# Output blocks of a fused attention and MoE kernel, copied out of PSUM by halves

## The chip, the cores and the metric

The kernel runs on one core of one Trainium2 chip. The metric is the device time of one execution in microseconds (us). The engines are PE (matmul), DVE (vector), ACT (scalar), POOL and SP; SP and ACT can issue DMAs, and PSUM is the memory that PE accumulates in and that ACT and DVE read.

## The reference

Sparse attention feeds two feed-forward layers. The part that matters here is the last one, on 1536 tokens, with `w_in` 512 x 2048 and `w_out` 2048 x 512:

```python
def _moe2_ref(x, w_in, w_out):
    h = x @ w_in
    g = h * (1.0 / (1.0 + np.exp(-h)))
    return (g @ w_out).astype(np.float32)
```

## The kernel before

An order written out by hand (`ORDER`) runs the attention and the first layer. The second layer then runs in two groups of 768 tokens, `g` = 0 and 1. For each of 16 slices `m` of 128 hidden features `up(g, m)` makes the activated slice: `up_mm` (L560) runs 24 matmuls into one PSUM tile, ACT takes the tanh (L569), DVE multiplies (L575), and a pair of ACT (L110) and DVE (L111) copies splits the result into a high part `gh` and a low part `gl`. `down(g, m)` (L611) multiplies that slice by its rows of `w_out`. It runs 18 matmuls: three token blocks `t3`, two halves `s` of the group, and three products each. PE works one step ahead: `up(g, m)` stands ahead of `down(g, m-1)`.

The sums over all 16 slices stay in three PSUM tiles, `acc[g][t3]`, each of 128 partitions x 2 x 512 f32. Half `s` of block `t3` is `acc[g][t3][:, s]`, and it holds 128 rows of the output. In the last slice the order is t3 outside, s inside, so that one tile after the other is finished. When both halves of a tile are done, ACT copies half 0 (L620) and DVE half 1 (L618) into `x2T`, an SBUF tile that is free by then, both times 0.5, and SP issues one DMA of 256 KB for each (L621). That is three tiles, six copies and six DMAs in each group.

In group 0 this stands behind `x2split(1)`, which makes the input of group 1: four ACT copies (`x2_hi`, L540) and four DVE subtractions (`x2_lo`, L543). Behind group 0 stands `up(1, 0)`. Behind group 1 stands the end of the program: each engine takes a branch (L714) around a fallback that isn't run here, and then waits for the others.

The program is built by a framework that inserts the semaphore waits itself: a write to a tile waits for the earlier readers of that tile. The engines run their instructions in the order in which they were written.

Of the kernel before, what the change touches and what calls it, by code (L numbers as in the profile page):

```python
# [13 lines left out]
ACTF = mybir.ActivationFunctionType  # L14
ALU = mybir.AluOpType
# [41 lines left out]
def kernel(ctx, tc, q, k, v, n_global, n_local, w_in, w_out, g_ln, w2_in, w2_out, out):  # L57
    nc = tc.nc
    B, H, S, D = 2, 8, 768, 64
    NT, DM = out.shape  # L60
# [16 lines left out]
    x2T = per.tile([128, KD, NT], F32, name="x2T")  # L77
# [28 lines left out]
    def psum():  # L106
        return ps.tile([128, 2, 512], F32, tag="p", name="p")
# [409 lines left out]
    G = 768  # L517
    HG = 384
    NG = NT // G
# [10 lines left out]
    for i in range(NP):  # L530
# [4 lines left out]
        for j in range(2):  # L535
            r = (2 * i + j) * 128
# [61 lines left out]
    acc = {}  # L598

    def down(g, m):  # L600
        if m == 0:
            acc[g] = [psum() for _ in range(G // 256)]
        last = m == KF2 - 1
        gx = [gs.pop((g, m, s)) for s in range(2)]
        ST = [(s, t3) for t3 in range(3) for s in range(2)] if last else [(s, t3) for s in range(2) for t3 in range(3)]
        for s, t3 in ST:
            hi, lo = gx[s]
            o = acc[g][t3][:, s]
            c = slice(t3 * 128, (t3 + 1) * 128)
            for i, (x, w) in enumerate(((hi, w3h), (hi, w3l), (lo, w3h))):  # L610
                nc.tensor.matmul(o, lhsT=x[:, c], rhs=w[m // 2][:, m % 2, :], start=(m == 0 and i == 0), stop=(last and i == 2))  # L611
            if last and s:
                for h in range(2):
                    r = g * G + (3 * h + t3) * 128
                    o = acc[g][t3][:, h]
                    y = x2T[:, r // 384, r // 128 % 3 * DM:(r // 128 % 3 + 1) * DM]
                    if h:
                        nc.vector.tensor_scalar(out=y, in0=o, scalar1=0.5, scalar2=None, op0=ALU.mult)  # L618
                    else:
                        nc.scalar.activation(out=y, in_=o, func=ACTF.Copy, scale=0.5)  # L620
                    nc.sync.dma_start(out=out[r:r + 128, :], in_=y)  # L621

    def guard():
        V = nc.vector
# [53 lines left out]
    with tc.manual_schedule():  # L678
# [18 lines left out]
        for i in range(2, NP):  # L697
            w2alloc(w2b, i)
        bg(2)
        down(0, 0)  # L700
        for m in range(2, KF2):
            up(0, m, 2)
            down(0, m - 1)
        x2split(1)
        down(0, KF2 - 1)
        for m in range(KF2):
            up(1, m)
# [6 lines left out]
    with tc.If(fast == 0):  # L714
# [12 lines left out]
        with tc.tile_pool(name="ga", bufs=1, side="left") as ga:  # L727
# [17 lines left out]
            with tc.For_i(0, B, 1) as bi, tc.For_i(0, H, 1) as hi:  # L745
                t3 = ga.tile([128, TB, D], F32, name="gv")
# [9 lines left out]
                for qb in range(TB):  # L756
# [31 lines left out]
                    o = psum()[:, 0, 0:D]  # L788
# [115 lines left out]
```

## Time and profile before

| | us |
|---|---|
| median of 3 runs | 517.35 (517.03 to 517.89) |
| the profiled execution | 515.7 |
| its span, from the first to the last instruction | 513.9 |
| PE busy in it | 485.1 (94%) |
| DVE, ACT, POOL busy in it | 312.6, 254.3, 111.9 |

The span is 1.8 us shorter than the time of the same execution, and that execution was 1.65 us faster than the median. A row of the timeline gives the start, the duration, the engine, the line, the operation and the tiles; what stands in brackets is the idle time ahead of it and what ended that. Ends of matmuls are modelled.

### The profile page before, as it was taken

What the parts mean: (1) busy time and instruction counts of PE and PEld (TensorE: products, weight loads), DVE (VectorE), ACT (ScalarE), POOL (GpSimd) and SP (SyncE); (2) the same over time, 40 slices, a digit from 0 to 9 for tenths busy, and PEclk for the clock granted to TensorE, in tenths of its full rate; (3) what the DMA queues carried; (4) which work ended last, traced back from release to release, by engine and by line L of the source; (5) the groups of instructions that cost most, each with busy time, mean ns of one, the idle gap of its engine ahead of it and who ended that gap; (6) DMA issues with size and microseconds to landing.
All of it is one profiled execution on the core that took longest, in us unless ns stands there. A gap on an engine that the chain in (4) does not pass through costs nothing.

```text
span 513.9 us, 8122 instructions
## 1 busy us (share of the span) xinstructions
PE 485.1 (94%) x3028; PEld 432.4 (84%) x3028; DVE 312.6 (61%) x735; ACT 254.3 (49%) x580; POOL 111.9 (22%) x150
## 2 busy tenths in 40 slices
PE   2598999999999999999999999999999999999993
PEld 1376779889888998799989899998899899999982
DVE  5799999956585686862688989893541313222231
ACT  3798997765666575442254545443431222222121
POOL 3675333311012133320223333332000000000000
PEclk9989999999999999999999999999999999999997
DMA  8757251612111210200333333300020000000003
GB/s 263 243 153 218 86 165 42 226 43 82 29 36 43 102 42 12 73 14 30 94 113 122 124 128 119 122 2 0 21 103 1 0 1 0 1 1 1 0 1 129
DMA packets 26179, 38.36 MB, mean 75 GB/s; under 512 B 1548, under 2 KB 13844, under 8 KB 26132
## 3 DMA queue, kind: packets, MB, share of 16 engines
q1 hardware_dynamic: 24932, 36.71, 22.0%
q10 hardware_dynamic: 1200, 1.05, 0.7%
q8 instruction: 26, 0.43, 0.3%
q14 instruction: 21, 0.17, 0.1%
HBM read 34.61 MB, written 3.15 MB: 73 GB/s over the span
## 4 chain that ended last, share of the span: by engine, by line
PE 85%; DVE 8%; DMA 2%; ACT 1%; issue 1%; POOL 0%; SPq 0%; DVEq 0%
PE p L560 26%; PE p L611 26%; PE p L497 12%; PE p L413 9%; PE p L308 4%; PE p L355 3%; PE p L374 3%; PE p L477 2%; DVE A L327 2%; DMA rq<-in_q_dram 1%; DMA rk<-in_k_dram 1%; DVE cc L147 1%; DVE cc L145 1%; DVE cc L143 1%; ACT A L333 1%
## 5 line engine op out<-in xcount | busy, mean ns | idle before, releaser
L575 DVE SCALAR_TENSOR_TENSOR e<-e,p 128x384 f32<-128x384 f32 x64 | 32.6, 551 | 127.5 <-ACT e L569 127.5
L569 ACT ACTIVATE e<-p 128x384 f32<-128x384 f32 x64 | 28.0, 490 | 129.5 <-PE p L560 129.5
L611 PE MATMUL p<-w3h,gl 128*128 128x512 f32 x192 | 75.3, 392 | 0.0
L611 PE MATMUL p<-w3l,gh 128*128 128x512 f32 x192 | 75.2, 392 | 0.0
L611 PE MATMUL p<-w3h,gh 128*128 128x512 f32 x192 | 74.7, 389 | 0.0
L147 DVE SCALAR_TENSOR_TENSOR cc<-cx,cc 128x512 uint32<-128x512 uint32 x48 | 60.9, 1270 | 0.3
L560 PE MATMUL p<-x2h,w2h 128*128 128x384 f32 x256 | 55.2, 337 | 0.0
L560 PE MATMUL p<-x2l,w2h 128*128 128x384 f32 x256 | 55.0, 335 | 0.0
L560 PE MATMUL p<-x2h,w2l 128*128 128x384 f32 x256 | 54.7, 334 | 0.0
L333 ACT ACTIVATE A<-A,negmax 128x256 f32<-128x256 f32 (+1 forms) x96 | 46.0, 481 | 13.3 <-DVE negmax L327 11.7
L413 PE MATMUL p<-wih,xT 128*128 128x512 f32 x192 | 50.6, 405 | 0.5 <-DVE negmax L327 0.5
L327 DVE CUSTOM_DVE_ANT_0 A<-p,bias 128x256 f32<-128x256 f32 (+1 forms) x96 | 34.3, 395 | 23.1 <-PE p L355 14.6
L560 PEld LDWEIGHTS p<-x2h,w2h 128*128 128x128 f32 x256 | 45.6, 188 | 2.3
L560 PEld LDWEIGHTS p<-x2l,w2h 128*128 128x128 f32 x256 | 45.9, 188 | 0.0
L560 PEld LDWEIGHTS p<-x2h,w2l 128*128 128x128 f32 x256 | 45.3, 188 | 0.0
L611 PEld LDWEIGHTS p<-w3h,gl 128*128 128x128 f32 x192 | 36.0, 188 | 7.6
L611 PEld LDWEIGHTS p<-w3l,gh 128*128 128x128 f32 x192 | 36.0, 188 | 6.9
L611 PEld LDWEIGHTS p<-w3h,gh 128*128 128x128 f32 x192 | 36.1, 188 | 6.8
L413 PEld LDWEIGHTS p<-wih,xT 128*128 128x128 f32 x192 | 34.3, 189 | 8.5 <-DVE negmax L327 0.9
L110 ACT ACTIVATE gh<-e 128x384 fp32r<-128x384 f32 x60 | 29.7, 526 | 18.6 <-DVE e L575 18.6
L145 DVE SCALAR_TENSOR_TENSOR cc<-cx,cc 128x512 uint32<-128x512 uint32 x48 | 34.1, 716 | 0.0
L111 DVE TENSOR_TENSOR gl<-e,gh 128x384 fp32r<-128x384 f32 x60 | 30.8, 555 | 3.8
(117 smaller groups left out, 804.9 us busy)
## 6 DMA issues: line engine op xcount, KB each, us to landing
cx<-in_moe_w_out_dram SPq DMA_DIRECT2D x24, 512.0 KB, 3.4
cx<-in_moe_w_in_dram SPq DMA_DIRECT2D x23, 512.0 KB, 3.7
rq<-in_q_dram SPq DMA_DIRECT2D x12, 256.0 KB, 6.1
vf<-in_v_dram SPq DMA_DIRECT2D x12, 256.0 KB, 4.5
out_dram<-x2T SPq DMA_DIRECT2D x12, 256.0 KB, 2.7
rk<-in_k_dram SPq DMA_DIRECT2D x10, 256.0 KB, 5.6
rk<-in_k_dram ACTq DMA_DIRECT2D x2, 256.0 KB, 4.8
cx<-in_moe_w_in_dram ACTq DMA_DIRECT2D x1, 512.0 KB, 6.2
```

The source lines that it names most:

```text
L110: nc.scalar.activation(out=hi, in_=src, func=ACTF.Copy)
L111: nc.vector.tensor_tensor(out=lo, in0=src, in1=f(hi), op=ALU.subtract)
L145: V.scalar_tensor_tensor(out=y, in0=x[:, :, 0].bitcast(U32), scalar=29, in1=y, op0=ALU.logical_shift_right, op1=ALU.bitwise_or)
L147: V.scalar_tensor_tensor(out=y, in0=x[:, :, 1].bitcast(U32), scalar=0x80000000, in1=y, op0=ALU.bitwise_and, op1=ALU.bitwise_or)
L327: nc.vector.tensor_tensor_reduce(out=x[:, c, 0:n], in0=p[:, a, j, 0:n], in1=bb, scale=-0.125, scalar=1e30, op0=ALU.add, op1=ALU.min, accum ...
L333: nc.scalar.activation(out=x[:, c, 0:n], in_=x[:, c, 0:n], func=ACTF.Exp, bias=negmax[:, t * H + h:t * H + h + 1], scale=-1.0, accum_out=s ...
L413: nc.tensor.matmul(p[:, half, :], lhsT=x[:, a, kk, :], rhs=w[:, kk, n], start=(i == 0), stop=(i == 11))
L497: nc.tensor.matmul(p[:, d], lhsT=x[:, kk, c], rhs=y[:, kk, sl], start=(i == 0), stop=(i == 3 * KF - 1))
L560: nc.tensor.matmul(p, lhsT=w[m // 2][:, kk, c], rhs=x[:, kk, s * HG:(s + 1) * HG], start=(i == 0), stop=(i == 11))
L569: nc.scalar.activation(out=e, in_=p2[:, s, 0:HG], func=ACTF.Tanh, scale=0.5)
L575: nc.vector.scalar_tensor_tensor(out=e, in0=e, scalar=1.0, in1=p2[:, s, 0:HG], op0=ALU.add, op1=ALU.mult)
L611: nc.tensor.matmul(o, lhsT=x[:, c], rhs=w[m // 2][:, m % 2, :], start=(m == 0 and i == 0), stop=(last and i == 2))
```

## The change

In the last slice each half is copied right after its own three matmuls. Half 0 goes to ACT and half 1 to DVE, as before. The very last half of the program (group 1, t3 = 2, s = 1) is cut by columns: ACT copies the first 256, DVE the other 256. A DMA is issued by ACT where ACT copied and by SP where DVE copied. The number of DMAs goes from 12 to 13.

```diff
-            if last and s:
-                for h in range(2):
-                    r = g * G + (3 * h + t3) * 128
-                    o = acc[g][t3][:, h]
-                    y = x2T[:, r // 384, r // 128 % 3 * DM:(r // 128 % 3 + 1) * DM]
-                    if h:
-                        nc.vector.tensor_scalar(out=y, in0=o, scalar1=0.5, scalar2=None, op0=ALU.mult)
+            if last:
+                end = g == NG - 1 and t3 == 2 and s == 1
+                r = g * G + (3 * s + t3) * 128
+                y = x2T[:, r // 384, r // 128 % 3 * DM:(r // 128 % 3 + 1) * DM]
+                for n, act in ((slice(0, 256), True), (slice(256, DM), False)) if end else ((slice(0, DM), s == 0),):
+                    if act:
+                        nc.scalar.activation(out=y[:, n], in_=o[:, n], func=ACTF.Copy, scale=0.5)
                     else:
-                        nc.scalar.activation(out=y, in_=o, func=ACTF.Copy, scale=0.5)
-                    nc.sync.dma_start(out=out[r:r + 128, :], in_=y)
+                        nc.vector.tensor_scalar(out=y[:, n], in0=o[:, n], scalar1=0.5, scalar2=None, op0=ALU.mult)
+                    (nc.scalar if act else nc.sync).dma_start(out=out[r:r + 128, n], in_=y[:, n])
```

On PE, in the last slice of group 1, tile t3 = 1 (`p_3966`; `gh_4753` and `gl_4754` belong to half 0, `gh_4757` and `gl_4758` to half 1):

```order
 L611 MATMUL p_3966<-w3l7_2820,gh_4753 128x512
 L611 MATMUL p_3966<-w3h7_2819,gl_4754 128x512
-L611 MATMUL p_3966<-w3h7_2819,gh_4757 128x512
+L611 MATMUL p_3966<-w3h7_2819,gh_4757 128x512 [waits Activation_49]
 L611 MATMUL p_3966<-w3l7_2820,gh_4757 128x512
 L611 MATMUL p_3966<-w3h7_2819,gl_4758 128x512
```

No matmul has moved, but the first one of half 1 now waits for ACT. The same stands at t3 = 2 and in group 0. At t3 = 0 that matmul had a wait for ACT already (for `gh`); it now waits for a later ACT instruction, the copy.

On ACT, the end of group 1 (`p_3965`, `p_3966`, `p_3967` are the tiles of t3 = 0, 1, 2; `DMAHW` is a DMA's completion semaphore):

```order
-L620 ACTIVATE x2T_62<-p_3965 128x512 [waits PE_49]
-L620 ACTIVATE x2T_62<-p_3966 128x512 [waits PE_49]
-L620 ACTIVATE x2T_62<-p_3967 128x512 [waits PE_49]
+L618 ACTIVATE x2T_62<-p_3965 128x512 [waits PE_49]
+L621 DMA out_0_dram<-x2T_62 128x512 [waits Activation_49]
+L618 ACTIVATE x2T_62<-p_3966 128x512 [waits PE_49]
+L621 DMA out_0_dram<-x2T_62 128x512 [waits DMAHW7_49,Activation_49]
+L618 ACTIVATE x2T_62<-p_3967 128x512 [waits PE_49]
+L621 DMA out_0_dram<-x2T_62 128x512 [waits DMAHW1_49,Activation_49]
+L618 ACTIVATE x2T_62<-p_3967 128x256 [waits PE_49]
+L621 DMA out_0_dram<-x2T_62 128x256 [waits DMAHW2_49,Activation_49]
```

ACT has a DMA behind each copy, and one copy and one DMA more.

On DVE at the same place:

```order
-L618 TENSOR_SCALAR x2T_62<-p_3965 128x512 [waits Activation_49]
-L618 TENSOR_SCALAR x2T_62<-p_3966 128x512 [waits Activation_49]
-L618 TENSOR_SCALAR x2T_62<-p_3967 128x512 [waits Activation_49]
+L620 TENSOR_SCALAR x2T_62<-p_3965 128x512 [waits PE_49,Activation_49]
+L620 TENSOR_SCALAR x2T_62<-p_3966 128x512 [waits PE_49,Activation_49]
+L620 TENSOR_SCALAR x2T_62<-p_3967 128x256 [waits Activation_49]
```

The last one is half as long and still waits for ACT alone, by its count for the 128x256 copy just ahead of it in program order.

## Rows read from the trace of the kernel before

**Rows 1.** The page: busy us, share of the span and instructions by engine.
```profile
PE 485.1 (94%) x3028; PEld 432.4 (84%) x3028; DVE 312.6 (61%) x735; ACT 254.3 (49%) x580; POOL 111.9 (22%) x150
```

**Rows 2.** The page: the chain that ended last, by engine.
```profile
PE 85%; DVE 8%; DMA 2%; ACT 1%; issue 1%; POOL 0%; SPq 0%; DVEq 0%
```

**Rows 3.** Busy time by stretch: length, then PE, PEld, DVE, ACT, POOL; clock, DMA, GB/s.
```profile
214.00:505.90 291.90, 291.88 (x1555) 267.40 (x1553) 147.32 (x233) 101.72 (x200) 39.00 (x28) 1.00 0.14 46
```

**Rows 4.** The chain in order of time, from 480 us on: start, length, what.
```profile
497.67 8.22 PE p L611 x36
...
505.91 0.61 ACT x2T L620
...
506.54 0.69 DVE x2T L618
```

**Rows 5.** Timeline of SP: the fifth store of group 1; the fifth and sixth merged.
```profile
506.54 1.56 SPq L621 DMA_DIRECT2D out_dram<-x2T  x1
...
506.54 2.07 SPq L621 DMA_DIRECT2D out_dram<-x2T  x2
```

**Rows 6.** Instructions of L621 and L714: ns min/median/max, first and last start.
```profile
L621 SPq DMA_DIRECT2D out_dram<-x2T x12: 332/343/1558, 371.0 to 508.2; - x12
...
DMA to landing us min/median/max: 2.0/2.7/4.1
...
L714 SPq COMPARE_BRANCH  x1: 50/50/50, 508.7 to 508.7; - x1
```

**Rows 7.** Waits of SP from 505 us on: us in total, times, longest.
```profile
SPq L714 <- SPq L714: 3.3, 1, 3.3
```

**Rows 8.** Groups by form: 128x256 copies out of PSUM; busy, mean ns.
```profile
L128 ACT ACTIVATE x2T<-p 128x256 f32<-128x256 f32 x17 | 6.1, 379 | 11.9 <-PE p L497 11.3 <-DVE x2T L130 0.7
...
L130 DVE TENSOR_SCALAR x2T<-p 128x256 f32<-128x256 f32 x7 | 2.8, 418 | 5.2 <-PE p L497 5.2
```

**Rows 9.** Timeline, tile t3 = 0 of group 1: its last matmul, the next, the copy.
```profile
502.77 0.39 PE L611 MATMUL p<-w3h,gl 128*128 128x512 f32 x1
...
502.99 0.39 PE L611 MATMUL p<-w3h,gh 128*128 128x512 f32 x1
...
503.19 0.60 ACT L620 ACTIVATE x2T<-p 128x512 f32<-128x512 f32 x1 [3.00 <-PE p L611]
```

**Rows 10.** Timeline: PE released by the end of an ACT instruction.
```profile
211.07 1.24 ACT L465 ACTIVATE e<-e,st 128x1024 f32<-128x1024 f32 x1 [0.56 <-POOL st L460]
...
212.36 1.09 PE L477 MATMUL p<-ident,e 128*128 128x128 f32 x8 [1.21 <-ACT e L465]
```

**Rows 11.** Timeline of PE: a first 128x512 matmul after a wait; the next two.
```profile
35.52 0.50 PE L413 MATMUL p<-wih,xT 128*128 128x512 f32 x1 [0.46 <-DVE negmax L327]
...
35.86 0.63 PE L413 MATMUL p<-wih,xT 128*128 128x512 f32 x2
```

**Rows 12.** Timelines of PE, ACT and DVE around the end of group 0.
```profile
369.25 0.39 PE L611 MATMUL p<-w3h,gl 128*128 128x512 f32 x1
...
367.26 3.04 ACT L540 ACTIVATE x2h<-x2T 128x768 fp32r<-128x768 f32 x4
370.35 0.60 ACT L620 ACTIVATE x2T<-p 128x512 f32<-128x512 f32 x1
...
368.12 3.56 DVE L543 TENSOR_TENSOR x2l<-x2T,x2h 128x768 fp32r<-128x768 f32 x4 [0.18 <-ACT x2h L540]
```

**Rows 13.** Timeline of ACT: two DMAs that ACT issues at the start.
```profile
0.74 0.43 ACTq L208 DMA_DIRECT2D rk<-in_k_dram  x1
1.20 0.53 ACTq L123 DMA_DIRECT2D cx<-in_moe_w_in_dram  x1
```

**Rows 14.** Busy time by stretch, columns as in Rows 3.
```profile
23.96:26.50 2.54, 0.00 (x0) 0.00 (x0) 2.44 (x10) 2.44 (x8) 1.85 (x3) 1.00 0.55 151
26.70:30.10 3.40, 3.40 (x18) 3.07 (x17) 3.40 (x7) 3.28 (x7) 3.40 (x4) 0.50 0.61 174
...
38.00:43.00 5.00, 3.19 (x22) 2.46 (x21) 4.93 (x8) 4.58 (x9) 3.82 (x5) 1.00 0.92 303
```

## The prediction

> **What bounds the kernel now.** I read the page first: PE is busy for 485.1 of 513.9 us [rows 1], and it holds 85% of the chain that ended last [rows 2]. An average says nothing of the stage that is changed, so I read that stage next: from 214 us to 505.9 us PE is busy for 291.88 of 291.90 us [rows 3]. There is no gap in which a delay of PE could hide. Whatever holds PE up by one microsecond anywhere in these 292 us makes the program one microsecond longer. The copies of ACT and DVE lie beside it and cost nothing, except for the very last ones.
>
> Third, the end. PE's last matmul ends at 505.89 (497.67 + 8.22), then ACT copies until 506.52, and only then DVE from 506.54 to 507.23 [rows 4]. SP has two stores to issue after PE's end. The first took 1.56 us to issue, where the median is 0.34, so that the second, which had its data at 507.23, was through at 508.61 (506.54 + 2.07) [rows 5, 6]. SP takes its branch at 508.7 [rows 6], which holds it for 3.3 us [rows 7], and the span ends at 513.9, 5.3 us behind that last issue. The last data land within this time: a landing takes 2.0 to 4.1 us from the issue [rows 6]. So the tail is 2.72 us from PE's last matmul to the end of SP's last issue, and a fixed 5.3 us behind it.
>
> **What the change removes.** Let M be the end of PE's last matmul. ACT starts 0.02 us later [rows 4], copies 128x256 in 0.38 [rows 8], DVE starts 0.02 later [rows 4] and takes 0.42 [rows 8], and SP issues 0.02 after that (506.54 against 506.52) in 0.33 [rows 4 to 6]: M + 1.19. The tail gets 2.72 - 1.19 = 1.53 us shorter. Of this 1.23 (1.56 less 0.33) is the slow issue, which then no longer stands ahead of the last one on SP, since ACT issues for itself. The cut itself saves less than it seems: DVE's piece waits for ACT's piece in the built program, so the two run one after the other, 0.38 + 0.42 against 0.60 + 0.69. If they ran side by side, the tail would gain another 0.4; if SP's last issue took 1.56 again, it would gain only 0.30. I take 1.53, since a store of 256 KB every 0.7 us stood ahead of the slow issue and one every 1.1 us or more will stand ahead of this one.
>
> The Trainium skill ("PSUM — Partial Sum Buffer", section "PSUM bank collisions raise a hardware error") states that two engines reading one PSUM bank at once collide, even in different columns. By that, the two pieces of one half couldn't run side by side in any build; no run here shows it.
>
> **What the change adds.** The first matmul of half 1 writes the same PSUM tile from which ACT reads half 0, and the built program makes it wait until that copy is done. There are three tiles in each of two groups, so this happens six times. PE has nothing to do meanwhile: it runs in order, and the next tile's matmuls stand behind the waiting one.
>
> One such wait is put together from four rows. ACT starts its copy 0.42 us after the start of the third matmul of the half (502.77 to 503.19) [rows 9]. The copy takes 0.60 [rows 9]. PE goes on 0.05 after ACT's end (211.07 + 1.24 = 212.31, PE at 212.36) [rows 10]. Before, the next matmul started 0.22 after the third [rows 9]. So PE is late by 0.42 + 0.60 + 0.05 - 0.22 = 0.85. Then there is the weight load: after a wait, the first 128x512 matmul runs for 0.50, and the next one starts 0.34 after it [rows 11], 0.11 or 0.12 more than in a running row, because its weights weren't loaded beside an earlier matmul. Together I take 0.95 us. The bounds are 0.84, if the load is hidden after all, and 1.1, if release and restart both come out a little longer than in these rows.
>
> At one of the six it is more. In group 0 ACT still makes x2h (L540) until 370.30 [rows 12]. The third matmul of t3 = 0, half 0, starts at 369.25 [rows 12]; the copy can't start before 370.3, ends at 370.93 (its row of before gives 370.35 + 0.60 = 370.95), and PE goes on at 370.98 instead of 369.47. That is 1.51 + 0.1 = 1.61 us. The copy of t3 = 1 overwrites columns that x2_lo (L543) reads, but the first of its four instructions is done about 0.95 us after 368.12 [rows 12], so that wait is met.
>
> ACT's DMA issues stand behind its copies: three in group 0, four in group 1. The nearest rows are 0.43 and 0.53 us [rows 13], and the far one is SP's 1.56 [rows 5]. From the end of one copy to the next ACT has about 1.7 us (0.05 restart, 0.34 + 0.23 + 0.23 for half 1, 0.45 to the third matmul of the next tile, 0.42). Even 1.56 would just fit, so I cost them at nothing; without that cover an issue would go onto PE's wait in full. On SP six issues of twelve fall away, which only waited for data. The stores start earlier and are spread over a longer time, and none is waited for before the end.
>
> The sum, against the profiled execution's own 515.7 us (span 513.9 and 1.8 around it): group 0 adds 1.61 + 0.95 + 0.95 = 3.51, group 1 adds 3 x 0.95 = 2.85, the tail takes off 1.53. That is +4.83, or 520.5 us. The median of the runs shown is 1.65 above that execution, so on its scale the forecast is 517.35 + 4.83 = **522.2 us**.
>
> **The rivals.**
>
> *PE doesn't really wait (not slower).* The place is the first matmul of half 1. If the copy were over by the time PE comes there, the stalls would vanish and the tail's gain would be left: 517.35 - 1.53 = 515.8 us. The change is a gain from a mean stall of less than 1.53 / 6 = 0.26 us on. Against it: the copy alone takes 0.60 [rows 9] and can't begin before the half's last matmul has ended, while the waiting matmul stands right behind that one. Chance 5%, of which 2 are for a partial form that ends within 0.2% of before.
>
> The Trainium skill ("PSUM — Partial Sum Buffer", section "Summary: rules for kernel authors") advises to read another bank than the one being written and to guard by bank. By that rule the halves, a bank each, needn't wait for one another, and the time would be this rival's 515.8. The waits of the built program speak against it: the guard in them is by tile.
>
> *The clock falls (slower still).* After PE had been idle for 2.54 us (23.96 to 26.50), the granted clock was 0.50, that is 1.2 GHz, for 3.40 us [rows 14]. If the three stalls at the end of group 0 did the same, half of 3.40, 1.7 us, would be lost: 523.9. Against it: from 38 to 43 us PE was busy for 3.19 of 5.00 us, and the clock stayed at 1.00, 2.4 GHz [rows 14]; at the end of group 0 it would be busy for about 4.1 of 7.6. Chance 7%.
>
> *SP's last issue is slow again.* It would cost 1.56 - 0.33 = 1.23: 523.4. For it: the issue comes as soon after PE's end as the slow one did. Against it: the slow one is the maximum of twelve with a median of 0.34 [rows 6], and this queue then holds half as many stores. Chance 10%.
>
> **How the numbers follow.** The forecast has 78%, the three rivals 5, 7 and 10. Low end: six waits of 0.84, the extra of group 0 gone, and both pieces of the last half side by side: 5.04 - 1.93 = +3.1, 520.5. High end: five waits of 1.1 and one of 1.75, and a tail gain of only 0.30: +6.95, 524.3; I set 524.2. The two slower rivals lie inside as well; that is more than 8 in 10, but the bounds of the costs are no tighter than this. Within 0.2% (1.03 us, about what a measurement of this kernel can tell from no change) comes only from the partial form of the first rival: 2%. Faster 3%, slower 95%.
>
> **What would show it.** In the profile after: six waits of PE p L611 for ACT x2T, five with 0.65 to 0.7 us of idle (0.42 + 0.60 + 0.05 less the matmul's 0.39) and one near 1.35; PE no longer fully busy from 214 us on; the last slice of group 1 some 2.9 us longer than 4.1; SP's last issue over 1.2 us after PE's end; ACT's issues near 0.4 us, and no PE wait that grows with them. The forecast is wrong if PE's waits are missing or below 0.3 us, if the tail stays at 2.7 us, or if PE waits at another place, such as the first `up` of group 1.

## The result

| | before | changed |
|---|---|---|
| median, first comparison | 517.19 us (516.49 to 517.89, 4 runs) | 520.40 us (520.18 to 521.00, 4 runs) |
| median, second comparison | 516.19 us (514.52 to 517.60, 17 runs) | 520.62 us (520.17 to 522.71, 6 runs) |
| the profiled execution, its span | 515.7, 513.9 | 520.18, 518.4 |

The change makes the kernel slower: by the first comparison 1.0063 times the time (95% interval 1.0048 to 1.0078, that is 2.5 to 4.0 us), by the second 1.0091 (1.0068 to 1.0114, 3.5 to 5.9 us). The profiled executions differ by 4.5 us. The forecast was 522.2, with 520.5 as its low end; 520.4 lies 0.1 below that. The sign and the mechanism came out as forecast, the time on the scale of the median did not.

The waits of PE from 214 us on in the changed kernel (columns: us in total, times, longest). Before there was none [rows 3]:

```profile
PE p L611 <- ACT x2T L618: 4.6, 6, 1.2
```

Six waits, and no other. Two of them in the timeline of PE, the first in group 0 and the first in group 1 (columns as in the rows of before):

```profile
369.30 0.39 PE L611 MATMUL p<-w3h,gl 128*128 128x512 f32 x1
370.87 0.50 PE L611 MATMUL p<-w3h,gh 128*128 128x512 f32 x1 [1.19 <-ACT x2T L618]
371.21 0.39 PE L611 MATMUL p<-w3l,gh 128*128 128x512 f32 x1
...
505.56 0.39 PE L611 MATMUL p<-w3h,gl 128*128 128x512 f32 x1
506.63 0.50 PE L611 MATMUL p<-w3h,gh 128*128 128x512 f32 x1 [0.69 <-ACT x2T L618]
506.97 0.40 PE L611 MATMUL p<-w3l,gh 128*128 128x512 f32 x1
```

From the start of the third matmul of the half to the start of the next it is 1.07 us in group 1 (505.56 to 506.63) where it was 0.22 [rows 9]. The waiting matmul runs for 0.50 and the next starts 0.34 after it, just as after a wait of another kind in the trace of before [rows 11]. ACT at the same places:

```profile
367.31 3.03 ACT L540 ACTIVATE x2h<-x2T 128x768 fp32r<-128x768 f32 x4
370.25 0.57 ACT L618 ACTIVATE x2T<-p 128x512 f32<-128x512 f32 x1
370.85 0.36 ACTq L621 DMA_DIRECT2D out_dram<-x2T  x1
...
505.98 0.60 ACT L618 ACTIVATE x2T<-p 128x512 f32<-128x512 f32 x1 [2.31 <-PE p L611]
506.61 0.34 ACTq L621 DMA_DIRECT2D out_dram<-x2T  x1
508.32 0.60 ACT L618 ACTIVATE x2T<-p 128x512 f32<-128x512 f32 x1 [1.74 <-PE p L611]
```

The first copy waited behind x2h, as forecast. ACT's DMA issue takes 0.34 to 0.36 us and is over long before the next copy can start. The chain that ended last, from 501 us on, with the "issue" pieces left out:

```profile
501.14 4.82 PE p L611 x21
505.98 0.60 ACT x2T L618
...
506.63 1.67 PE p L611 x6
508.32 0.60 ACT x2T L618
...
508.97 1.67 PE p L611 x6
510.66 0.60 ACT x2T L618
511.31 0.98 PE p L611 x3
512.31 0.39 ACT x2T L618
512.73 0.42 DVE x2T L620
```

The copies that lay beside PE [rows 4] now stand between its matmuls, three times in this group. The last two lines show the cut of the last half: 0.39 on ACT and only then 0.42 on DVE. SP and its branch in the changed kernel:

```profile
510.76 2.75 SPq L621 DMA_DIRECT2D out_dram<-x2T  x2
```

```profile
L621 ACTq DMA_DIRECT2D out_dram<-x2T x7: 338/339/357, 370.9 to 512.7; - x7
L621 SPq DMA_DIRECT2D out_dram<-x2T x6: 332/332/348, 372.7 to 513.2; - x6
...
L714 SPq EVENT_SEMAPHORE  x8: 17/17/17, 516.5 to 517.0; - x8
...
L714 SPq COMPARE_BRANCH  x1: 45/45/45, 513.6 to 513.6; - x1
```

SP's last issue ends at 513.51 (510.76 + 2.75), 1.24 us after PE's last matmul (512.27); before it was 2.72 [rows 4, 5]. No issue is slow any more. Behind the branch SP goes on after 2.9 us (513.6 to 516.5), before after 3.3 [rows 7].

### The profile page after: what moved, and what is told of

The parts are those of the page before. It is cut to its first block, busy times and chain, and to the rows that moved or that the text cites. A ratio compares the mean times of both kernels' runs of the same rounds, so it can differ in the third digit from the quotient of the medians.

```text
span 518.4 us, 8127 instructions
## 1 busy us (share of the span) xinstructions
PE 486.9 (94%) x3028; PEld 431.9 (83%) x3028; DVE 312.3 (60%) x735; ACT 254.5 (49%) x581; POOL 112.1 (22%) x150
## 3 DMA queue, kind: packets, MB, share of 16 engines
q10 hardware_dynamic: 2208, 2.75, 1.7%
## 4 chain that ended last, share of the span: by engine, by line
PE 84%; DVE 8%; ACT 3%; DMA 2%; issue 1%; POOL 0%; SPq 0%; DVEq 0%
PE p L560 26%; PE p L611 25%; PE p L497 12%; PE p L413 9%; PE p L308 3%; PE p L355 3%; PE p L374 3%; PE p L477 2%; DVE A L327 2%; DVE cc L147 1%; DMA rk<-in_k_dram 1%; DVE cc L145 1%; DMA rq<-in_q_dram 1%; DVE cc L143 1%; ACT x2T L618 1%
## 5 line engine op out<-in xcount | busy, mean ns | idle before, releaser
L611 PE MATMUL p<-w3h,gh 128*128 128x512 f32 x192 | 75.4, 393 | 4.6 <-ACT x2T L618 4.6
L611 PE MATMUL p<-w3h,gl 128*128 128x512 f32 x192 | 75.4, 392 | 0.0
L611 PE MATMUL p<-w3l,gh 128*128 128x512 f32 x192 | 75.3, 392 | 0.0
L560 PE MATMUL p<-x2h,w2h 128*128 128x384 f32 x256 | 55.2, 337 | 0.0
L560 PE MATMUL p<-x2l,w2h 128*128 128x384 f32 x256 | 55.0, 336 | 0.0
L560 PE MATMUL p<-x2h,w2l 128*128 128x384 f32 x256 | 54.7, 334 | 0.0
L413 PE MATMUL p<-wih,xT 128*128 128x512 f32 x192 | 50.6, 405 | 0.5 <-DVE negmax L327 0.5
L611 PEld LDWEIGHTS p<-w3h,gh 128*128 128x128 f32 x192 | 36.1, 188 | 13.8 <-ACT x2T L618 7.2
L560 PEld LDWEIGHTS p<-x2h,w2h 128*128 128x128 f32 x256 | 45.6, 188 | 2.3
L560 PEld LDWEIGHTS p<-x2l,w2h 128*128 128x128 f32 x256 | 45.9, 188 | 0.0
L560 PEld LDWEIGHTS p<-x2h,w2l 128*128 128x128 f32 x256 | 45.3, 188 | 0.0
L611 PEld LDWEIGHTS p<-w3h,gl 128*128 128x128 f32 x192 | 36.0, 188 | 7.6
L611 PEld LDWEIGHTS p<-w3l,gh 128*128 128x128 f32 x192 | 36.0, 188 | 6.7
L413 PEld LDWEIGHTS p<-wih,xT 128*128 128x128 f32 x192 | 34.4, 189 | 8.5 <-DVE negmax L327 0.9
```

Of the source, the lines that this page charges most:

```text
L413: nc.tensor.matmul(p[:, half, :], lhsT=x[:, a, kk, :], rhs=w[:, kk, n], start=(i == 0), stop=(i == 11))
L560: nc.tensor.matmul(p, lhsT=w[m // 2][:, kk, c], rhs=x[:, kk, s * HG:(s + 1) * HG], start=(i == 0), stop=(i == 11))
```

## The experiments

Most of what follows reads three points of each trace: the start of the first matmul of `down` (everything ahead of it is the same in all kernels, except in the two with other PSUM pools), the modelled end of PE's last matmul, and the end of the span.

| kernel | first `down` | last matmul ends | span ends | between the first two | tail |
|---|---|---|---|---|---|
| before | 248.39 | 505.88 | 513.88 | 257.49 | 8.00 |
| before, second profile | 250.38 | 507.86 | 515.74 | 257.48 | 7.88 |
| before, third profile | 250.85 | 508.33 | 515.32 | 257.48 | 6.99 |
| changed | 248.44 | 512.27 | 518.40 | 263.83 | 6.13 |
| changed, again (1) | 249.78 | 513.62 | 519.78 | 263.84 | 6.16 |
| a tile for every half (2) | 250.90 | 510.74 | 517.34 | 259.84 | 6.60 |
| pair tiles, the same pools (3) | 249.43 | 515.65 | 521.48 | 266.22 | 5.83 |
| early copies, one queue, no cut (4) | 249.14 | 513.01 | 518.99 | 263.87 | 5.98 |
| second queue alone (5) | 249.47 | 506.95 | 514.30 | 257.48 | 7.35 |
| early copies in group 1 alone (6) | 248.63 | 509.06 | 515.09 | 260.43 | 6.03 |
| halves in the order of other slices (7) | 249.49 | 508.11 | 514.62 | 258.62 | 6.51 |
| the version without stalls (8) | 250.37 | 507.85 | 514.83 | 257.48 | 6.98 |

The column "between" repeats to 0.01 us where the code is the same. The first column and the tail don't: the first varies by 2.5 us.

**1. The changed kernel again.** No edit.

> The changed kernel once more, to measure the difference with more rounds. The two profiles differ by 4.5 us in span (518.4 against 513.9), the medians by only 3.2. Theory A (the profiled execution of before was an early draw of a distribution that both kernels have): the difference of the medians stays anywhere from 3 to 4.5 and the spread of both is alike. Theory B (before has something in most executions, worth 1 to 1.5 us, that its profile did not show and that the change takes away, most likely in its tail): the difference stays at 3.2 +- 0.5, before spreads over more than 1 us, and the changed kernel over less.

Measured: 520.62 us, beside 516.19 for 17 runs of before in the same comparison. The difference is 4.4 us, as the profiles have it, and before spreads over 3.1 us, the changed kernel over 2.5. This speaks for theory A, that the 3.2 us of the first comparison were a matter of four runs; the intervals of the two comparisons overlap. Between its two points the second profile of the changed kernel has 263.84 us, the first 263.83.

**2. A PSUM tile for every half.** A new PSUM pool of six single accumulators and one tile for the `up` matmuls, opened ahead of group 0:

```diff
-            acc[g] = [psum() for _ in range(G // 256)]
+            acc[g] = [[psa.tile([128, 512], F32, tag="a", name="a", bufs=6) for _ in range(2)] for _ in range(G // 256)]
...
-            o = acc[g][t3][:, s]
+            o = acc[g][t3][s]
```

> The changed kernel with a PSUM tile of its own for every half (six 128x512 accumulators in place of three 128x2x512); nothing else moves. Theory 'the guard is by tile': the six waits of PE for ACT vanish, PE's last matmul ends near 506 us as before, and the tail is that of the changed kernel, 6.1 us to the span's end: span 512.0 to 512.4, 1.5 to 1.9 us faster than before by the profiles. Theory 'the engines cannot share PSUM at that moment anyway': the waits or a slower copy stay, and the time stays 3 us above before.

Measured: 519.30 us (6 runs), 1.0056 (1.0035 to 1.0077) of before. That is 3.1 us slower than before, where 1.5 to 1.9 us faster was expected. The waits of PE from 214 us on (L612 and L561 are L611 and L560 of the other kernels):

```profile
PE p L561 <- DVE e L576: 2.0, 1, 2.0
PE p L478 <- ACT e L466: 1.2, 1, 1.2
PE a L612 <- DVE x2T L131: 0.9, 1, 0.9
```

The six waits for the copies are gone, as the theory had it, and the copies of ACT take 0.60 us as before while PE writes the next half. But I had overlooked what the pool costs: with one tile left for `up`, PE waits 2.0 us between the first two `up` of group 1, and 0.9 us where the pools change. (The wait of 1.2 us is in the first layer and in all kernels.) So the time alone decides nothing here, and the next run is its control.

**3. The same pools with pair tiles.**

```diff
-            acc[g] = [[psa.tile([128, 512], F32, tag="a", name="a", bufs=6) for _ in range(2)] for _ in range(G // 256)]
+            acc[g] = [psa.tile([128, 2, 512], F32, tag="a", name="a", bufs=3) for _ in range(G // 256)]
```

> The control for the run with a PSUM tile for every half: the same new PSUM pools (so the same two waits of 0.9 and 2.0 us that come from having one tile for the `up` matmuls), but the accumulators are pairs again, 128x2x512. Theory 'the guard is by tile': the six waits of PE for ACT are back, and the kernel is 6.2 +- 0.4 us slower than the run with a tile for every half (2.0 of the 6.35 could shrink only if a wait falls under another one). Theory 'the pools made the difference': the two are equal.

Measured: 523.96 us (4 runs), 1.0168 (1.0141 to 1.0194) of before. Its waits:

```profile
PE a L612 <- ACT x2T L619: 4.6, 6, 1.2
PE p L561 <- DVE e L576: 2.0, 1, 2.0
PE a L612 <- DVE x2T L131: 0.9, 1, 0.9
```

The two waits of the pools are the same, the six for the copies are back with their 4.6 us. Between its two points it has 266.22 us, the run with a tile for every half 259.84: 6.38 us for the guard by tile. (Their medians stand only 4.7 apart; the two ran on different chips, and the profiles of the two differ by 1.5 in the first column and by 0.8 in the tail.) Theory "by tile" holds: the halves don't disturb each other in PSUM, the wait comes from their sharing a tile.

**4. Early copies alone, one queue, the last half whole on DVE.**

```diff
-                for n, act in ((slice(0, 256), True), (slice(256, DM), False)) if end else ((slice(0, DM), s == 0),):
+                for n, act in ((slice(0, DM), s == 0),):
...
-                    (nc.scalar if act else nc.sync).dma_start(out=out[r:r + 128, n], in_=y[:, n])
+                    nc.sync.dma_start(out=out[r:r + 128, n], in_=y[:, n])
```

> Only the early copying by halves: all DMAs on SP, and the last half whole on DVE. The six waits of PE stay. Theory 'the tail is shorter because the halves are spread over a longer time': the slow issue of 1.56 us does not come back, the last copy and issue take 0.02 + 0.69 + 0.02 + 0.33 = 1.06 us, and the time is that of the changed kernel or 0.2 us less. Theory 'the second queue is what shortens the tail': SP's last issue is slow again, and the time is 1.2 us above the changed kernel.

Measured: 520.96 us (6 runs), 1.0095 (1.0076 to 1.0114) of before, beside 520.62 for the changed kernel in the same comparison. SP's issues of the stores:

```profile
L621 SPq DMA_DIRECT2D out_dram<-x2T x12: 332/332/348, 371.5 to 513.8; - x12
```

All twelve on one queue, and none is slow. The tail is 5.98, 0.15 shorter than that of the changed kernel. So beside the early copies the second queue and the cut together shorten nothing. PE's stalls pull the stores apart, which may be why none is slow; of the runs with early copies and without the long stalls (2, 7 and 8) two have a slow issue and one has none, so this is not shown.

**5. The second queue alone.**

```diff
-                    nc.sync.dma_start(out=out[r:r + 128, :], in_=y)
+                    (nc.sync if h else nc.scalar).dma_start(out=out[r:r + 128, :], in_=y)
```

> Only the second queue: copies in pairs after both halves, as before, the last half whole, but ACT issues the DMAs of what it copied. PE has no waits. Theory 'the tail is 1 us shorter through the queue': the end of SP's last issue is 0.02 + 0.60 + 0.02 + 0.69 + 0.02 + 0.33 = 1.68 us after PE's end instead of 2.72, 1.0 us faster than before by the profile. Theory B above (most executions of before lose another 1 to 1.5 us in the tail): 2 us or more faster than before's median. Third possibility: ACT's or SP's issue is slow as before, no change.

Measured: 515.81 us (12 runs), 0.9993 (0.9980 to 1.0005) of before: no difference clear of the runs' spread. The issues became even, as the first theory had it, but the tail is only 0.65 shorter than that of the first profile of before (8.00 to 7.35), and longer than that of the third (6.99):

```profile
L621 ACTq DMA_DIRECT2D out_dram<-x2T x6: 338/339/380, 372.1 to 507.6; - x6
L621 SPq DMA_DIRECT2D out_dram<-x2T x6: 332/332/348, 373.4 to 508.3; - x6
...
DMA to landing us min/median/max: 2.0/2.8/4.3
```

Landings still take up to 4.3 us. SP's last issue starts at 508.3, so a landing of that length comes as late as 512.6, when SP is back from its branch. The waits of SP from 505 us on show that it waited for them, here and in the changed kernel:

```profile
SPq L714 <- SPq L714: 3.8, 3, 2.9
```

```profile
SPq L714 <- SPq L714: 2.9, 1, 2.9
```

In both, one wait of 2.9 us is the branch. The second queue alone has two more, 0.9 us together: its last two stores land at 512.38 and 512.54, and SP goes on at 512.40 and 512.56. So SP's last issue ends 1.0 us earlier after PE's end than in the first profile of before, as expected (1.72 against 2.72), and the landings then end the program in place of the queue.

**6. Early copies in group 1 alone.** Group 0 copies in pairs as before.

```diff
-            if last:
+            if last and (s or g == NG - 1):
+                for h in (range(2) if g < NG - 1 else (s,)):
...
```

> The change in group 1 alone; group 0 copies in pairs as before. If the stalls of the two groups simply add, this takes the 3.45 us of group 0 back: 1.0 us above before (2.9 of stalls less 1.9 of tail), 3 to 4 us below the changed kernel. If PE loses something else in group 0 (a clock that falls, a late `up`), the difference is another.

Measured: 517.41 us (10 runs), 1.0025 (1.0007 to 1.0044) of before, which is +0.9 against 516.48. Between its points it has 260.43 us, so group 1 costs 2.95 and group 0 the other 3.40 of the changed kernel's 6.35. The stalls add.

**7. The halves in the order of the other slices.** Early copies, second queue and cut as in the changed kernel.

```diff
-        ST = [(s, t3) for t3 in range(3) for s in range(2)] if last else [(s, t3) for s in range(2) for t3 in range(3)]
+        ST = [(s, t3) for s in range(2) for t3 in range(3)]
```

> The changed kernel with the last slice in the order of the other slices: half 0 of all three tiles first, then half 1. The copy of a tile's half 0 then has 6 matmuls of other tiles (1.36 us) to hide under. In group 0 ACT is free only from 370.3 on and has DMA issues between its copies, so some 0.5 to 0.7 us of waiting stays; in group 1 at most 0.3 us. With the tail of the changed kernel (1.87 us shorter): 0.8 to 1.3 us faster than before. If the order makes no difference to the waits, it stays 4.4 above before.

Measured: 516.40 us (10 runs), 1.0012 (0.9995 to 1.0029) of before. It is 4 us faster than the changed kernel by this one line, but not faster than before, where 0.8 to 1.3 us was expected. In the stretch around the end of group 0 (columns as in rows 3)

```profile
368.00:376.00 8.00, 7.82 (x35) 5.86 (x34) 6.67 (x9) 5.06 (x8) 0.00 (x0) 1.00 0.35 132
```

PE is busy for 7.82 of 8.00 us, where the changed kernel's was for 4.84 of the 7.40 us from 369.0 to 376.4. Some waiting is left: between its points it has 258.62 us, 1.13 more than before, a little over what I had expected, because here ACT's DMA issues do stand in the way of its next copy. In group 0:

```profile
371.02 0.39 PE L611 MATMUL p<-w3h,gl 128*128 128x512 f32 x1
...
371.29 0.58 ACT L618 ACTIVATE x2T<-p 128x512 f32<-128x512 f32 x1
...
371.90 0.36 ACTq L621 DMA_DIRECT2D out_dram<-x2T  x1
...
372.36 0.60 ACT L618 ACTIVATE x2T<-p 128x512 f32<-128x512 f32 x1 [0.49 <-PE p L611]
...
373.01 0.50 PE L611 MATMUL p<-w3h,gh 128*128 128x512 f32 x1
```

The half that ACT copies from 372.36 on was finished at 371.41 (371.02 + 0.39). ACT comes to it 0.49 us after its last copy, with the issue in between, and PE's next matmul on that tile starts behind the copy's end. The tail is the other part of the miss: it is 6.51 us and not the 6.13 of the changed kernel, since SP's last issue took 0.98 us:

```profile
L621 SPq DMA_DIRECT2D out_dram<-x2T x6: 332/338/977, 373.7 to 509.0; - x6
```

**8. A version without stalls.** Group 0 as before. In group 1 half 0 of all tiles first, each half copied as it finishes, all DMAs on SP except the last, and the last half whole on ACT, which issues its DMA. Parts of the edit of the kernel before:

```diff
-        ST = [(s, t3) for t3 in range(3) for s in range(2)] if last else [(s, t3) for s in range(2) for t3 in range(3)]
+        ST = [(s, t3) for t3 in range(3) for s in range(2)] if last and g < NG - 1 else [(s, t3) for s in range(2) for t3 in range(3)]
...
-                    if h:
+                    if h and not end:
                         nc.vector.tensor_scalar(out=y, in0=o, scalar1=0.5, scalar2=None, op0=ALU.mult)
                     else:
                         nc.scalar.activation(out=y, in_=o, func=ACTF.Copy, scale=0.5)
-                    nc.sync.dma_start(out=out[r:r + 128, :], in_=y)
+                    (nc.scalar if end else nc.sync).dma_start(out=out[r:r + 128, :], in_=y)
```

> A version meant to beat both: group 0 in pairs as before, group 1 with half 0 of all tiles first and early copies, all DMAs on SP except the last one, and the last half whole on ACT, which issues its DMA. No wait of PE for a copy. ACT's last issue would end 0.02 + 0.60 + 0.02 + 0.34 = 0.98 us after PE's end, SP would be through before that: 2 to 2.4 us faster than before if the branch behind the last issue decides, 1 to 1.5 if the landing of the last 256 KB does (late landings came up to 5.6 us after PE's end in the run with only the second queue).

Measured: 515.06 us (12 runs), 0.9982 (0.9969 to 0.9995) of before, between 0.3 and 1.6 us faster. PE from the first `down` on:

```profile
250.40:507.80 257.40, 257.40 (x1298) 233.43 (x1296) 130.36 (x203) 89.44 (x177) 36.37 (x25) 1.00 0.15 50
```

No stall. The tail is 1.0 shorter than that of the first profile of before, and as long as that of the third (6.98 and 6.99). SP's waits from 505 us on:

```profile
SPq L715 <- SPq L715: 4.7, 3, 3.3
```

Behind the branch (3.3 us) SP waits 1.4 us more, until the last two stores have landed at 512.92 and 513.08. So landings end this kernel, the second form of the expectation (1 to 1.5 us faster); the medians differ by 1.4. It is the only one of the kernels whose interval lies wholly below the time of before.

**9 and 10. The kernel before, profiled twice more.**

> The kernel before, profiled a second time. Theory A (the executions differ in the first stage, where loads are waited for, and the end is alike): the first matmul of the last stage's `down` starts anywhere from 248.4 to 250.4 us, and from PE's last matmul to the span's end it is again 8.0 +- 0.3 us with one slow DMA issue on SP. Theory B (the end varies): the first part is as in the first profile, and the end differs by 1 us or more.

> The same a third time, with the same two expectations, since one execution can't tell a spread.

Measured: 517.64 and 517.14 us. The first matmul of `down`, in the first, second and third profile:

```profile
248.39 0.40 PE L611 MATMUL p<-w3h,gh 128*128 128x512 f32 x1
```

```profile
250.38 0.40 PE L611 MATMUL p<-w3h,gh 128*128 128x512 f32 x1
```

```profile
250.85 0.40 PE L611 MATMUL p<-w3h,gh 128*128 128x512 f32 x1
```

SP's issues in the second and the third:

```profile
L621 SPq DMA_DIRECT2D out_dram<-x2T x12: 332/398/1456, 373.0 to 510.1; - x12
```

```profile
L621 SPq DMA_DIRECT2D out_dram<-x2T x12: 332/338/753, 373.4 to 509.7; - x12
```

Both theories have a part. The stretch ahead of `down` gives 2.5 us of spread, and the tail 1.0 us: the third execution had no issue longer than 0.75 us and a tail of 6.99. The first profile, on which the prediction stood, had the earliest first `down` and the longest tail of the three.

Of the 2.5 us, 0.6 go with the clock. In the first and the second profile (columns as in rows 3):

```profile
43.00:46.40 3.40, 3.40 (x31) 2.67 (x31) 3.40 (x17) 1.94 (x5) 1.79 (x3) 1.00 1.03 303
```

```profile
43.00:46.40 3.40, 3.40 (x13) 3.01 (x13) 3.40 (x12) 2.95 (x6) 2.25 (x4) 0.50 1.00 308
```

In the second (and in the third, from 43.5 us on) the granted clock fell once more to 0.50, that is 1.2 GHz, which it did not do there in the first. From the first matmul of L413 (35.52, 36.89 and 37.34 us) to the first `down` it is 212.87, 213.49 and 213.51 us. The other 1.4 to 1.8 us lie ahead of that matmul.

## Why the prediction was right and where it was wrong

- **PE's six waits: right, and in size.** The sum was 3.51 + 2.85 = 6.36 us. The traces give 263.83 - 257.49 = 6.34, and 6.35 in the second profile of the changed kernel. Five waits show 0.69 us of idle (forecast 0.65 to 0.7), the first 1.19 (near 1.35), since ACT began its copy at 370.25 rather than after 370.3 and took 0.57 us. The restart of 0.34 or 0.35 is there in each.
- **The guard by tile: right.** One tile for each half takes the waits away, and pair tiles in the same pools bring them back, 6.38 us. So the rival "PE doesn't really wait" was the right picture of a kernel that this change doesn't make. The rule of the Trainium skill that the prediction weighed ("PSUM — Partial Sum Buffer", section "Summary: rules for kernel authors": read another bank than the one being written) agrees with that run, where ACT's copies take 0.60 us and PE waits for none of them.
- **The tail: near, but not a fixed term.** The forecast took 1.53 off; the two profiles differ by 8.00 - 6.13 = 1.87. SP's last issue ended 1.24 us after PE's end (forecast 1.19). The part behind it, which the prediction called fixed at 5.3 us, was 4.9, because SP came back from its branch in 2.9 us and not 3.3. It isn't fixed in the kernel before either: against the second and the third profile of before the gain is 1.75 and 0.86 us. So that the sum met the first pair of profiles so closely is in part luck.
- **What the tail's gain is due to: partly wrong.** The prediction put 1.23 of it down to the second queue. The run with early copies on one queue has the same tail, so on top of the early copies the queue and the cut bring nothing; and the second queue alone gained nothing that the times show, since landings took the place of the issues. That the cut pieces run one after the other came out as forecast (0.39, then 0.42 us).
- **The step that failed: "The median of the runs shown is 1.65 above that execution, so on its scale the forecast is 517.35 + 4.83 = 522.2 us."** On its own scale the sum gave 520.5 us, and the profiled execution of the changed kernel took 520.18, its medians 520.40 and 520.62. So the changed kernel's median lay 0.22 above its profiled execution (0.44 in the second comparison), where the forecast added 1.65. Of the 1.8 us between 522.2 and 520.40 this term makes 1.43 and the sum 0.35. The 1.65 was no property of the kernel. The runs of before reach from 514.52 to 518.43 (29 runs, median 516.48), and the median of three lay 0.9 above that of the 29; in the two larger comparisons the median of before lies only 0.49 and 0.78 above 515.7. The three profiles of before show where executions differ: 2.5 us ahead of `down`, 1.0 us in the tail, 0.01 between. That both profiled executions of the first comparison were early ones (first `down` at 248.39 and 248.44) is luck too. The stretch that the change touches is the steadiest of all, and I added an offset that comes from the others. The range had the same error at its low end: from the profiled execution it would have begun 1.65 lower, at 518.8.
- **The other rivals.** The clock didn't fall at the stalls: from 214 us to the end of PE's work it was 1.00 in the changed kernel too.

```profile
214.00:512.27 298.27, 293.65 (x1555) 266.98 (x1554) 147.38 (x233) 102.24 (x201) 39.28 (x28) 1.00 0.14 47
```

  PE is idle for 4.62 of these 298.27 us. But the row that the prediction set against this rival, a clock of 1.00 with PE busy for 3.19 of the 5.00 us from 38 to 43 [rows 14], was no safe sign: in the second profile of before PE was busy for 3.19 us in the same stretch, and there the clock was 0.50 from 43.0 us on. And SP's last issue was not slow again (0.33 us).

What stays open: why an issue takes 1.5 us. It happened to the fifth store in two profiles of before out of three (1.56 and 1.46 us), in the run with a tile for every half to ACT's last issue (1.70 us), and less so to SP's last with the halves in the order of other slices (0.98 us); in all of these the stores ahead of the slow issue stood less than 0.9 us apart. But so they did in the third profile of before, with the second queue alone and in the version without stalls, and there none took more than 0.75.

## What to carry to other kernels

Before a copy is moved ahead of work that is still to come, look whether that work writes the same tile: a copy that starts earlier gains nothing where the next matmul has to wait for it, and each wait costs the whole copy, the signal both ways and a weight load. A copy beside other work is free as long as enough matmuls of other tiles stand between its half and the next write to its tile, so the order of the matmuls is worth more than the place of the copies. And a sum made from one profiled execution belongs on that execution's scale: the offset to the median of a few runs carries the scatter of stages that the change doesn't touch.

## What the hardware showed that I had not expected

- A wait of PE costs more than its idle time: the matmul that waited takes 0.50 us and the next follows after 0.34 or 0.35, in a row where 0.39 and 0.22 are the rule, six times alike.
- The branch at the end holds SP for 2.6 to 3.3 us, so a store that lands in this time costs nothing. Where the last issue comes earlier, SP waits for landings instead: 0.9 us with the second queue alone, 1.4 us in the version without stalls.
